# Six of 32 head pairs multiply float32 probabilities with v as loaded, sums of both heads inverted together, and a new order of work

## The chip, the cores and the metric

The kernel runs on one core of a Trainium2 chip. The metric is the device time of one execution in microseconds (us). The engines are TensorE (PE, and PEld for its weight loads), VectorE (DVE), ScalarE (ACT), GpSimd (POOL) and SyncE (SP), which issues the transfers.

## The reference

Attention with a decay, and behind it a token and channel mixer with residual additions:

```python
scores = (q @ k.T) / sqrt(64)
cum = cumsum(log(clip(f, 1e-4, 1)))
scores = where(causal, -1e9, scores + cum[:, None] - cum[None, :])
attn = exp(scores - max(scores)); attn /= sum(attn) + 1e-9
x = attn @ v                                    # 8 batches, 8 heads, 576 tokens, 64 wide
u = x + (relu(x.T @ w_tok1) @ w_tok2).T         # 576 -> 256 -> 576
out = u + relu(u @ w_ch1) @ w_ch2               # 512 -> 1536 -> 512
```

All of it is float32. The weights come as float64 words and are decoded on the chip.

## The kernel before

The 64 heads are worked in 32 pairs (`n2`); the heads of a pair sit on the two halves of the 128 partitions, so that matmuls with 64 rows of each can run side by side. Four pairs are one batch of 8 heads, and after every second pair half a batch goes through the mixer (`mixer`, `joint`, `tok2`, and in the second half `ch1` and `ch2`). The channels that the mixer leaves out are done after attention with late weights (`unit`, then `plain_up`, `plain_down`, and products with fewer multiplications).

Most products run in rounded float32 (F32R): an operand is split into a high part, rounded by a copy, and a low part, which is the subtraction of the two (`hi_act` L508 on ACT, `lo_dve` L517 on DVE, `lo_pool` L514 on POOL). One float32 product then becomes two or three rounded ones. The scores of the first four pairs (`FQ=4`) are the exception: they use q and k as loaded, in float32.

A pair goes through these steps. Scores by `score` (L768), six pieces a head, each with one more rounded product for the decay (`cd`). Row minima by `rmin` (L782, DVE). Exponentials with row sums by `expo` (L786, ACT). Per head, 1e-9 is added to the sums and they are inverted (`rec1` L812, `rec2` L815, DVE), and five instructions normalise the probabilities (`norm` L820, POOL). Transpositions in three groups (`trs` L838, PE). For each group and head a copy to the high part (L508, ACT) and a low part (L517, DVE) into `pt`. Then `avs` (L883) multiplies `pt` with `vv`, in which v's high and low parts stand side by side in 128 columns (split at L742 by ACT and L514 by POOL), high `pt` first and then low `pt`; the results for v's high and low parts land on two halves of the partitions, and a copy by ACT (L898) with an addition by DVE (L902) joins them in `xt`. The block of the first 64 tokens has a lone 64-column product per head (`low`, L871); the second head's must wait for the first's, and stands at the head of the third group.

Weights are decoded by `decode`: a scaling on ACT (L588), two shifts or masks on DVE (L592, L596), a multiplication (L600), an addition (L604, POOL for the early weights and DVE for the late), a last merge (L608), then high and low parts.

The order of each engine's work is a table of numbers (`ORDER`) written out beforehand. `Plan.run` takes the operations of each engine in just that order, and picks the buffers as they come free by its own cost figures; `PORT` tells it from which batch on an operation marked `port=True` (decode steps on DVE) and any operation on POOL are kept from overlapping in its reckoning. On the chip the engines wait for each other by semaphores alone.

Buffers matter in two places. `part` is four float32 tiles that `ch2` uses for results on their way out. And the weights of the late part take over the room of attention's tiles in two steps, `gate0` when `raw`, `hl`, `vr` and `pr` are done with, `gate1` for `vv`, `pt` and `xn`.

Of the kernel before, what the change touches and what calls it, by code (L numbers as in the profile page):

```python
# [1709 lines left out]
```

## Time and profile before

| | us |
|---|---|
| median of 3 runs | 1044.23 |
| lowest, highest | 1042.71, 1045.01 |
| profiled execution | 1044.65 |
| its span | 1042.9 |
| busy: PE, PEld | 989.0, 895.0 |
| busy: DVE, ACT, POOL | 866.4, 629.9, 441.3 |

Busy time is a union over the whole span. The stages differ: attention runs up to about 541 us, the late weights are decoded up to about 674 us, and the rest is products with them. So a share of the whole says little, and the rows below are taken by stretch. The granted clock is given as a share of 2.4 GHz; TensorE has two levels, 1.2 and 2.4 GHz, and 0.76 is a mean of both. Idle time of an engine is put down to what ended it.

### The profile page before, as it was taken

Reading aid. Unit: us, or ns where it says so; the run is one execution under the profiler, and the core shown is the slowest. Engines: PE = TensorE matmul, PEld = TensorE weight load, DVE = VectorE, ACT = ScalarE, POOL = GpSimd, SP = SyncE. Lnnn points to the kernel's source line nnn. Section 1 sums busy time; section 2 is a strip of 40 time slices with the busy share of each in tenths; the row PEclk is TensorE's granted clock in tenths of the full one; section 3 lists DMA queues with packets and bytes.
Section 4 is the critical chain, followed back from the end, with each engine's and each line's share of the span. In section 5 each row is a group of like instructions: output and inputs, shape, how many; then the busy total and the mean of one; then the engine's idle time right before and its main releaser. Section 6 shows DMA issues by size and latency. Waiting matters only on the chain.

```text
span 1042.9 us, 26969 instructions
## 1 busy us (share of the span) xinstructions
PE 989.0 (95%) x10030; PEld 895.0 (86%) x10030; DVE 866.4 (83%) x2221; ACT 629.9 (60%) x1582; POOL 441.3 (42%) x519
## 2 busy tenths in 40 slices
PE   7579899999999999999987999999999999999998
PEld 5468899999999999999987888888888888888887
DVE  7998988788787887879788999958967994996487
ACT  5768688898897988889884544524513431442242
POOL 6767758778686877867731000012002200110210
PEclk9668899999999999999997999999999999999999
DMA  5331123333432232332416989999799879988884
GB/s 187 113 104 56 36 68 106 94 96 104 139 93 104 70 120 71 92 110 85 139 60 212 334 268 334 310 308 349 218 315 320 299 235 308 315 256 250 266 301 147
DMA packets 125859, 192.78 MB, mean 185 GB/s; under 512 B 18976, under 2 KB 77088, under 8 KB 124704
## 3 DMA queue, kind: packets, MB, share of 16 engines
q1 hardware_dynamic: 125632, 190.91, 56.5%
q8 instruction: 79, 1.29, 0.5%
q14 instruction: 52, 0.43, 0.1%
q10 hardware_dynamic: 96, 0.15, 0.0%
HBM read 144.34 MB, written 46.66 MB: 183 GB/s over the span
## 4 chain that ended last, share of the span: by engine, by line
PE 78%; DVE 14%; ACT 4%; DMA 2%; issue 1%; POOL 0%; SPq 0%; DVEq 0%; ACTq 0%
PE bank L1349 18%; PE bank L883 8%; PE bank L768 7%; PE bank L1165 6%; PE bank L1166 6%; PE bank L1167 6%; PE bank L1232 6%; PE bank L1230 6%; PE bank L1231 6%; PE bank L838 4%; DVE pr L782 3%; DVE xt L902 2%; DVE d_g L592 1%; ACT pr L786 1%; DVE pt L517 1%
## 5 line engine op out<-in xcount | busy, mean ns | idle before, releaser
L820 POOL TENSOR_SCALAR pr<-pr,rec 128x576 f32<-128x576 f32 (+4 forms) x320 | 169.8, 551 | 104.6 <-DVE rec L815 85.3
L786 ACT ACTIVATE pr<-pr,nmin 64x64 f32<-64x64 f32 (+4 forms) x320 | 177.2, 559 | 19.2 <-DVE nmin L782 18.6
L517 DVE TENSOR_TENSOR pt<-bank,pt 128x512 fp32r<-128x512 f32 x192 | 124.8, 682 | 16.4 <-ACT pt L508 15.4
L782 DVE CUSTOM_DVE_ANT_0 pr<-bank,mask 128x320 f32<-128x320 f32 (+3 forms) x320 | 124.8, 426 | 5.6 <-PE bank L768 4.9
L883 PE MATMUL bank<-pt,vv 64*128 64x512 f32 (+7 forms) x1152 | 115.6, 335 | 4.6 <-DVE pt L517 4.5
L508 ACT ACTIVATE pt<-bank 128x512 fp32r<-128x512 f32 x192 | 105.2, 597 | 19.8 <-PE bank L838 14.5
L768 PE MATMUL bank<-hl 64*128 64x320 f32 (+4 forms) x1008 | 105.5, 307 | 5.0 <-DVE nmin L782 3.7
L883 PEld LDWEIGHTS bank<-pt,vv 64*128 64x128 f32 x1152 | 102.4, 197 | 7.2 <-DVE pt L517 6.1
L768 PEld LDWEIGHTS bank<-hl 64*128 64x128 f32 x1008 | 87.4, 188 | 8.8 <-DVE nmin L782 5.4
L838 PE MATMUL bank<-ident,pr 64*128 64x64 f32 x1536 | 70.8, 232 | 14.7 <-DVE nmin L782 6.4
L838 PEld LDWEIGHTS bank<-ident,pr 64*128 64x128 f32 x1536 | 64.1, 145 | 17.4 <-POOL pr L820 14.9
L508 ACT ACTIVATE hid<-h 128x480 fp32r<-128x480 f32 x77 | 45.8, 602 | 54.1 <-PE bank L1231 36.9
L768 PE MATMUL bank<-cd,sel 64*128 64x320 f32 (+4 forms) x384 | 74.0, 340 | 4.1 <-DVE cd L551 4.1
L902 DVE TENSOR_TENSOR xt<-bank,xt 64x512 f32<-64x512 f32 (+1 forms) x128 | 57.2, 453 | 24.3 <-ACT xt L898 21.7
L514 POOL TENSOR_TENSOR hl<-raw,hl 128x1152 fp32r<-128x1152 f32 x28 | 75.0, 2678 | 1.5
L1349 PE MATMUL bank<-xn,t1h 64*128 64x256 f32 x512 | 63.6, 313 | 2.9 <-DVE ring L517 1.9
L1258 POOL TENSOR_TENSOR d_g<-d_g 128x480 f32<-128x480 f32 x4 | 5.1, 1280 | 142.6 <-DMA d_g<-pd 127.6
L786 ACT ACTIVATION_READ_ACCUMULATOR pr<-pr,nmin 128x1 f32 (+1 forms) x320 | 62.6, 196 | 0.0
L1349 PE MATMUL bank<-ring,w2h 64*128 64x288 f32 x512 | 59.9, 297 | 1.6 <-DVE ring L520 1.5
L1349 PE MATMUL bank<-ring,w1h 64*128 64x288 f32 x512 | 59.5, 305 | 1.3 <-POOL ring L514 1.3
L508 ACT ACTIVATE ring<-xt 128x576 fp32r<-128x576 f32 (+3 forms) x64 | 39.3, 632 | 34.5 <-DVE xt L1429 19.4
L898 ACT ACTIVATE xt<-bank 64x64 f32<-64x64 f32 (+1 forms) x128 | 50.3, 404 | 16.3 <-PE bank L883 12.7
(241 smaller groups left out, 3076.0 us busy)
## 6 DMA issues: line engine op xcount, KB each, us to landing
pw<-wd SPq DMA_DIRECT2D x280, 256.0 KB, 4.1
raw<-in_qk SPq DMA_DIRECT2D x28, 576.0 KB, 3.9
d_raw<-in_w_ch SPq DMA_DIRECT2D x80, 128.0 KB, 3.7
...
```

The source lines that it names most:

```text
L508: nc.scalar.activation(out, in_, func, scale=scale)
L514: nc.gpsimd.tensor_tensor(out, in_, asf(hi), op=ALU.subtract)
L517: nc.vector.tensor_tensor(out, in_, asf(hi), op=ALU.subtract)
L768: nc.tensor.matmul(at(buf)[:, of : of + w], q, k, start=(x == 0), stop=(x == len(passes)))
L782: nc.vector.tensor_tensor_reduce(o, x, y, -1.0 / D**0.5, first, op0=ALU.add, op1=ALU.min, accum_out=c0[:m, col : col + 1])
L786: nc.scalar.activation(x, x, AF.Exp, bias=E["nmin"][sm][:m, t : t + 1], scale=-1.0, accum_out=E["sums"][sm][:m, t : t + 1])
L820: nc.gpsimd.tensor_scalar(x, x, E["rec"][sm][:m, t // 2, t % 2 : t % 2 + 1], 0.0, op0=ALU.mult, op1=ALU.add)
L838: nc.tensor.transpose(at(ps[s])[:, k * D : (k + 1) * D], at(pr)[r, x, :, :].rearrange("p a b -> p (a b)"), E["ident"][r, r])
L883: nc.tensor.matmul(at(av[s])[:, 512 - w :], at(vv)[r, vblk(j), :], at(pt)[r, z, c : c + w], start=(z, gi, i) == (0, 0, 0), stop=(z, gi, i) ...
L902: "DVE", d_dve(n), lambda ps=ps, o=o, n=n, f=f, xt=xt, me=me, pp=pp: nc.vector.tensor_tensor(at(xt)[me, pp, o : o + n], at(ps)[me, f : f + ...
L1165: nc.tensor.matmul(o, wt[:, 0, :], h_, start=(first and k == 0), stop=False, skip_group_check=True)
L1349: last[s] = nc.tensor.matmul(at(ps[s ^ z])[:, : width[0]], a, m, start=(z == 0 and i == 0), stop=(z == 1 and i == len(todo[s]) - 1), skip_ ...
```

## The change

Pairs 0 to 3, 30 and 31 (`FV`) skip the splitting of v and of the transposed probabilities. Each transposed group is copied once, by ACT, into a float32 tile `pf`, which is made of two of the four `part` tiles, so two groups have room at a time. `avs` multiplies it in float32 with `vr`, v as loaded, 64 columns wide, in one product where there were two; one copy by ACT brings the result to `xt`, and DVE's additions are gone.

In all pairs the sums of both heads stand in one tile and are inverted by one `rec1` and one `rec2`, for which the last exponential of either head must be done; all ten normalisations follow from them. The lone 64-column product of the second head moves from the head of the third group to its end.

`PORT` is 0, so the planner keeps port operations and POOL apart from the first batch on; some of its cost figures are new, and the order table of every engine is new.

```diff
 PRM = dict(
-    FILL=36, F1=2, FQ=4, n_raw=1, ...
+    FILL=36, F1=2, FQ=4, FV=(0, 1, 2, 3, 30, 31), n_raw=1, ...
-PORT = 6
+PORT = 0
 ORDER = dict(
     PE=(
-        "10:32 189 192 197 206 279 42 262 43 265 270 44 229 234 239 45 363 244 371 366 245:2 380 302 307 312 317:3 439 "
+        "10:36 195 187 190 204 246 249 263 254 225 228 234 231 235:2 284 287 333 341 350 336 293 290 294 392 295 400 "
...
-        fq = n2 < FQ
+        fq, fv = n2 < FQ, n2 in PRM["FV"]
...
-        p.op("ACT", d_act((2 * NS - 1) * D, False), lambda vv=vv, vr=vr: nc.scalar.activation(at(vv)[:, :, 0:D], at(vr), AF.Copy), ...)
-        p.op("POOL", d_ptt((2 * NS - 1) * D), lambda vv=vv, vr=vr: lo_pool(at(vv)[:, :, D:], at(vr), at(vv)[:, :, 0:D]), ...)
+        if not fv:
+            p.op("ACT", ...)
+            p.op("POOL", ...)
...
+        sm = n2 % 2
+        def rec1(sm=sm):
+            nc.vector.tensor_scalar(E["rec"][sm][:, :, :2], E["sums"][sm].rearrange("p (a b) -> p a b", b=3), 1e-9, None, op0=ALU.add)
...
+        p.op("DVE", 78, rec1, rd=[("sums", 2 * sm + s, t) for s in (0, 1) for t in range(NS)], wr=[("rec", sm)])
+        p.op("DVE", 136, rec2, wr=[("rec", sm)])
         for s in (0, 1):
-            p.op("DVE", 72, rec1, rd=[("sums", sm, t) for t in range(NS)], wr=[("rec", sm)])
-            p.op("DVE", 100, rec2, wr=[("rec", sm)])
             for t in (4, 3, 2, 1, 0):
-                p.op("POOL", d_pts(end[t], 1), lambda t=t, f=norm: f(t), rd=[("rec", sm)], wr=[(pr, s, t)], bufs=[pr])
+                p.op("POOL", d_pts(end[t], 1), lambda t=t, s=s, f=norm: f(t, s), rd=[("rec", sm)], wr=[(pr, s, t)], bufs=[pr])
...
-            ps, pt = [Buf("bk"), Buf("bk")], Buf("pt")
+            ps, pt = [Buf("bk"), Buf("bk")], Buf("pf" if fv else "pt")
...
+                if fv:
+                    o = lambda pt=pt, s=s: at(pt).rearrange("p (k s x) -> p k s x", s=2, x=D)[:, :, s, :]
+                    p.op("ACT", d_act(512), lambda src_=src_, o=o: nc.scalar.activation(o(), src_(), AF.Copy), rd=[ps[s]], wr=[(pt, 0, s)], bufs=[ps[s], pt])
+                    continue
...
+                Z, M = ((0,), D) if fv else ((0, 1), P)
+                def left(r, j):
+                    return at(vr)[r, vblk(j), :] if fv else at(vv)[r, vblk(j), :]
+                def right(b, r, z, c, w):
+                    return at(b)[r, c : c + w] if fv else at(b)[r, z, c : c + w]
...
-                if gi == 2:
-                    low(1)
                 for i, (j, c, w) in enumerate(seq):
-                    for z in (0, 1):
+                    for z in Z:
                         for s in (0, 1):
...
-                                at(av[s])[:, 512 - w :], at(vv)[r, vblk(j), :], at(pt)[r, z, c : c + w],
+                                at(av[s])[:M, 512 - w :], left(r, j), right(pt, r, z, c, w),
...
+                if gi == 2:
+                    low(1)
...
+                if fv:
+                    p.op(
+                        "ACT", d_act(n) + 60, lambda ps=ps, o=o, n=n, f=f, xt=xt, me=me, pp=pp: nc.scalar.activation(at(xt)[me, pp, o : o + n], at(ps)[:D, f : f + n], AF.Copy),
+                        rd=tok, wr=[(xt, 2 * pp + s, o)], bufs=[ps, xt],
+                    )
+                    continue
...
+    k["pf"] = [(("part", 2 * i), ("part", 2 * i + 1)) for i in (0, 1)]
```

How the new table moves instructions shows best in three places. The first is DVE in pair 0, where the sums of head 0 (`sums_85`) are inverted; `pr` are the probabilities of a pair, `nmin` its row minima, `d_g` weights in decode. Before:

```order
L812 TENSOR_SCALAR rec_89<-sums_85 128x3x2
L782 ISA pr_178,nmin_82<-bank_68,mask 64x64
L782 ISA nmin_82 64x1
L815 RECIPROCAL rec_89<-rec_89 128x3x2
L608 SCALAR_TENSOR_TENSOR d_g_161<-d_raw,d_g_161 128x256
L592 TENSOR_SCALAR d_g_162<-d_g_162 128x256
L782 ISA pr_178,nmin_82<-bank_64,mask 128x3x64
L782 ISA nmin_82 128x1
L596 TENSOR_SCALAR d_g_162<-d_g_162 128x256
```

On DVE at the same step of pair 0 now:

```order
L588 TENSOR_SCALAR d_g_162<-d_g_162 128x256
L596 SCALAR_TENSOR_TENSOR d_g_161<-d_raw,d_g_161 128x256
L592 TENSOR_SCALAR d_g_162<-d_g_162 128x256
L807 TENSOR_SCALAR rec_89<-sums_85 128x6x2
L810 RECIPROCAL rec_89<-rec_89 128x6x2
L778 ISA pr_176,nmin_83<-bank_64,mask 128x3x64
L778 ISA nmin_83 128x1
L778 ISA pr_176,nmin_84<-bank_65,mask 128x5x64
```

The inversion is twice as wide, it stands behind all row minima of pair 0 instead of between them, and it is followed by minima of pair 1 (`pr_176`). The second place is further down on DVE, where stood the first low halves of the probabilities (`pt`), between decode steps and minima of pair 1. Before:

```order
L600 SCALAR_TENSOR_TENSOR d_g_161<-d_raw,d_g_161 128x256
L782 ISA pr_179,nmin_84<-bank_66,mask 128x3x64
L782 ISA nmin_84 128x1
L517 TENSOR_TENSOR pt_182<-bank_63,pt_182 128x8x64
L592 TENSOR_SCALAR d_g_162<-d_g_162 128x288
L782 ISA pr_179,nmin_83<-bank_65,mask 128x3x64
L782 ISA nmin_83 128x1
L596 TENSOR_SCALAR d_g_162<-d_g_162 128x288
```

After the inversion of pair 1 DVE now goes on with decode and the minima of pair 2:

```order
L807 TENSOR_SCALAR rec_90<-sums_86 128x6x2
L810 RECIPROCAL rec_90<-rec_90 128x6x2
L604 SCALAR_TENSOR_TENSOR d_g_161<-d_raw,d_g_161 128x256
L596 SCALAR_TENSOR_TENSOR d_g_162<-d_raw,d_g_162 128x256
L778 ISA pr_175,nmin_82<-bank_70,mask 128x5x64
L778 ISA nmin_82 128x1
```

No low half stands there any more. The third place is PE in the middle of attention, behind the last score of pair 16 (`hl` are q and k, split; `cd,sel` the decay). Before:

```order
L768 MATMUL bank_64<-hl_177 128x192
L768 MATMUL bank_65<-hl_177 128x192
L768 MATMUL bank_64<-cd,sel 128x192
L768 MATMUL bank_65<-cd,sel 128x192
L883 MATMUL bank_63<-pt_182,vv_181 128x320
L883 MATMUL bank_68<-pt_182,vv_181 128x320
```

PE behind the last score of pair 16 now:

```order
L764 MATMUL bank_64<-hl_173 128x64
L764 MATMUL bank_65<-hl_173 128x64
L764 MATMUL bank_64<-cd,sel 128x64
L764 MATMUL bank_65<-cd,sel 128x64
L1365 MATMUL bank_70<-xn_182,t1h 128x256
L1365 MATMUL bank_68<-xn_182,t1h 128x256
L1365 MATMUL bank_70<-xn_182,t1l 128x256
L1365 MATMUL bank_68<-xn_182,t1l 128x256
```

Before, the multiplications of pair 15 by v followed at once, and 106 matmuls stood between that score and the first transposition of pair 16; now the mixer's token product and the transpositions of pair 15 come first, and 229 stand between.

## Rows read from the trace of the kernel before

**Rows 1.** Table by stretch: length, PE, PEld, DVE, ACT, POOL busy; clock, DMA.

```profile
0.00:15.00 15.00, 9.08 (x76) 5.91 (x76) 8.48 (x19) 5.00 (x7) 8.50 (x18) 1.00 0.65 214
15.00:116.00 101.00, 76.31 (x840) 66.31 (x840) 94.72 (x278) 76.54 (x214) 73.41 (x90) 0.76 0.28 88
116.00:541.00 425.00, 417.30 (x6596) 407.61 (x6598) 351.53 (x1173) 356.85 (x1003) 306.89 (x372) 0.99 0.30 97
541.00:674.00 133.00, 122.15 (x870) 106.31 (x869) 127.27 (x286) 64.89 (x129) 6.13 (x4) 0.95 0.86 279
674.00:1042.90 368.90, 364.12 (x1656) 308.83 (x1654) 284.44 (x469) 126.65 (x231) 46.32 (x36) 1.00 0.86 278
```

**Rows 2.** Chain that ended last, 0 to 116 us, its shares.

```profile
by line: DVE pr L782 14.0%; DVE d_g L592 11.6%; PE bank L883 11.2%; issue 5.8%; DVE d_g L600 5.5%; DVE pt L517 4.8%; DVE d_g L596 4.8%; DVE xt L902 4.5%; PE bank L768 4.2%; ACT pt L508 3.1%; DVE d_g L608 3.0%; DMA d_raw<-in_w_tok 2.6%; POOL
```

**Rows 3.** Timeline, 105 to 121 us: start, length, engine, line, instruction.

```profile
110.12 4.63 DVE L592 TENSOR_SCALAR d_g<-d_g 128x512 uint32<-128x512 uint32 x1
...
113.06 1.40 POOL L514 TENSOR_TENSOR vv<-vr,vv 128x576 fp32r<-128x576 f32 x1
...
116.00 1.19 PE L883 MATMUL bank<-pt,vv 64*128 64x320 f32 x16 [2.25 <-DVE pt L517]
```

**Rows 4.** Groups on DVE, 0 to 116 us: count, busy us, mean ns, idle.

```profile
L517 DVE TENSOR_TENSOR pt<-bank,pt 128x512 fp32r<-128x512 f32 x27 | 17.7, 678 | 0.2
L592 DVE TENSOR_SCALAR d_g<-d_g 128x256 uint32<-128x256 uint32 (+2 forms) x17 | 16.1, 947 | 5.6 <-ACT d_g L588 5.5
L600 DVE SCALAR_TENSOR_TENSOR d_g<-d_raw,d_g 128x256 f32<-128x256 uint32 (+2 forms) x16 | 11.9, 741 | 0.1
L596 DVE TENSOR_SCALAR d_g<-d_g 128x256 uint32<-128x256 uint32 (+2 forms) x16 | 8.8, 549 | 0.1
L608 DVE SCALAR_TENSOR_TENSOR d_g<-d_raw,d_g 128x256 uint32<-128x256 uint32 (+2 forms) x15 | 8.4, 561 | 0.0
L902 DVE TENSOR_TENSOR xt<-bank,xt 64x512 f32<-64x512 f32 (+1 forms) x16 | 7.1, 453 | 2.0 <-ACT xt L898 1.2 <-PE bank L871 0.7
...
L815 DVE RECIPROCAL rec<-rec 128x6 f32<-128x6 f32 x10 | 1.8, 181 | 0.0
```

**Rows 5.** DVE while POOL rests: timeline at 6 us; a group, 520 to 680.

```profile
6.64 0.29 DVE L592 TENSOR_SCALAR d_g<-d_g 128x256 uint32<-128x256 uint32 x1 [5.45 <-ACT d_g L588]
...
7.55 0.42 DVE L600 SCALAR_TENSOR_TENSOR d_g<-d_raw,d_g 128x256 f32<-128x256 uint32 x1
...
L600 DVE SCALAR_TENSOR_TENSOR tmp<-d_raw,tmp 128x512 f32<-128x512 uint32 x6 | 4.1, 684 | 0.0
```

**Rows 6.** Timeline of PE: float32 scores, then products with v.

```profile
60.61 0.60 PE L768 MATMUL bank<-xt 64*128 64x256 f32 x4
...
61.16 0.70 PE L768 MATMUL bank<-xt 64*128 64x320 f32 x4
...
62.18 0.80 PE L768 MATMUL bank<-xt 64*128 64x320 f32 x3 [0.16 <-DVE xt L902]
...
62.97 0.48 PE L768 MATMUL bank<-xt 64*128 64x192 f32 x3
...
404.13 0.36 PE L1349 MATMUL bank<-xn,t1h 64*128 64x256 f32 x2
...
405.70 0.31 PE L883 MATMUL bank<-pt,vv 64*128 64x320 f32 x1
...
408.93 0.35 PE L1349 MATMUL bank<-t2h,ring 64*128 64x288 f32 x2
```

**Rows 7.** Timeline around the normalisation of pair 16, 296 to 302 us.

```profile
296.51 2.56 POOL L820 TENSOR_SCALAR pr<-pr,rec 128x576 f32<-128x576 f32 x5 [0.54 <-DVE rec L815]
...
300.01 2.57 POOL L820 TENSOR_SCALAR pr<-pr,rec 128x576 f32<-128x576 f32 x5 [0.94 <-DMA raw<-in_qk]
...
302.00 0.65 PE L838 MATMUL bank<-ident,pr 64*128 64x64 f32 x16
```

More of the change, by code (lines that the diff above doesn't have):

```diff
@@ L313 @@
     START = dict(PE=3000, DVE=900, ACT=1900, POOL=1810, SP=700)
-    FIFO = ("ring", "xt", "part", "pr", "hl", "vv", "raw", "vr", "pt", "xn", "av", "hid", "hidB", "pw", "sg", "sg2", "uh", "uh2", "H", "st", "wq", "q", "rr", "g2", "d_raw", "d_g", "qf")
+    FIFO = ("ring", "xt", "part", "pr", "hl", "vv", "raw", "vr", "pt", "pf", "xn", "av", "hid", "hidB", "pw", "sg", "sg2", "uh", "uh2", "H", "st", "wq", "q", "rr", "g2", "d_raw", "d_g", "qf")
     def __init__(self):
@@ L488, in d_act @@
     def d_act(n, ps=True, ptr=0):
-        return 0.833 * n + (51 if ps else 93) + 93 * ptr + (130 if n > 512 else 0)
+        return 0.833 * n + (51 if ps else 93) + 93 * ptr + (130 if ps and n > 512 else 0)
     def d_dve(n, fast=False):
@@ L497, in d_ptt @@
     def d_ptt(n):
-        return 150 + 2.1 * n
+        return 145 + 2.157 * n
     def at(b):
@@ L542, in decay @@
             p.op("ACT", 900, lambda q=q: ld(nc.scalar, q), wr=[("f", q)], bufs=[w], lat=2500)
-        p.op("DVE", d_dve(S, True), lambda: nc.vector.tensor_scalar(row(0), row(0), 1e-4, 1.0, op0=ALU.max, op1=ALU.min), rd=[("f", q) for q in range(4)], wr=["f"], bufs=[w])
+        p.op("DVE", d_dve(S, True), lambda: nc.vector.tensor_scalar(row(0), row(0), 1e-4, 1.0, op0=ALU.max, op1=ALU.min), rd=[("f", q) for q in range(4)], wr=["f"], bufs=[w], port=True)
         p.op("ACT", d_act(S, False) + 1300, lambda: nc.scalar.activation(row(0), row(0), AF.Ln), wr=["f"], bufs=[w])
         p.op(
-            "DVE", d_dve(S), lambda: nc.vector.tensor_tensor_scan(row(1), row(0), row(2), 0.0, op0=ALU.add, op1=ALU.add),
-            rd=["f", "zero"], wr=["c"], bufs=[w],
+            "DVE", 1270, lambda: nc.vector.tensor_tensor_scan(row(1), row(0), row(2), 0.0, op0=ALU.add, op1=ALU.add),
+            rd=["f", "zero"], wr=["c"], bufs=[w], port=True,
         )
-        p.op("DVE", d_dve(S, True), lambda: nc.vector.tensor_scalar(E["cd"], row(1), 1.0, None, op0=ALU.mult), rd=["c"], wr=["cd"], bufs=[w])
+        p.op("DVE", d_dve(S, True), lambda: nc.vector.tensor_scalar(E["cd"], row(1), 1.0, None, op0=ALU.mult), rd=["c"], wr=["cd"], bufs=[w], port=True)
         p.op(
             "DVE", d_dve(S), lambda: nc.vector.scalar_tensor_tensor(E["cd"], asf(E["cd"]), E["lows"], row(1), op0=ALU.mult, op1=ALU.add),
-            rd=["c"], wr=["cd"], bufs=[w],
+            rd=["c"], wr=["cd"], bufs=[w], port=True,
         )
@@ L608, in s6 @@
             nc.vector.scalar_tensor_tensor(g, high, 0x80000000, g, op0=ALU.bitwise_and, op1=ALU.bitwise_or)
-        m2, m1 = (1.2, 1.1) if p.batch < PORT else (1.0, 1.0)
         p.op("ACT", d_act(w, False), s1, rd=rd, wr=[gb], bufs=[rb, gb])
-        p.op("DVE", d_dve(w, True) * (m2 if late else 1.8), s2, wr=[gb], bufs=[gb], port=True)
-        p.op("DVE", d_dve(w, True) * (m2 if late else 1.8), s3, rd=[gb], wr=[(gb, 1)], bufs=[gb], port=True)
-        p.op("DVE", d_dve(w) * (m1 if late else 1.3), s4, port=True, rd=rd, wr=[(gb, 1)], bufs=[rb, gb])
+        p.op("DVE", d_dve(w, True) , s2, wr=[gb], bufs=[gb], port=True)
+        p.op("DVE", d_dve(w, True) , s3, rd=[gb], wr=[(gb, 1)], bufs=[gb], port=True)
+        p.op("DVE", d_dve(w) , s4, port=True, rd=rd, wr=[(gb, 1)], bufs=[rb, gb])
         p.op("DVE" if late else "POOL", d_dve(w) if late else d_ptt(w), s5, port=True, rd=[(gb, 1)], wr=[gb], bufs=[gb])
@@ L785, in expo @@
             m, x = size[t], prob(t, s)
-            nc.scalar.activation(x, x, AF.Exp, bias=E["nmin"][sm][:m, t : t + 1], scale=-1.0, accum_out=E["sums"][sm][:m, t : t + 1])
+            nc.scalar.activation(x, x, AF.Exp, bias=E["nmin"][sm][:m, t : t + 1], scale=-1.0, accum_out=E["sums"][sm // 2][:m, sm % 2 * (NS + 1) + t : sm % 2 * (NS + 1) + t + 1])
         for ts in ((4,), (5,), (3, 0), (2, 1)):
@@ L796, in build @@
                     p.op(
-                        "DVE", d_dve(where[0][t][3]), lambda t=t, s=s, sm=sm, f=rmin: f(t, s, sm), rd=[ps[s]] + ([("nmin", sm, NS)] if t == 5 else []),
+                        "DVE", d_dve(where[0][t][3]) + 68 * (t == 5), lambda t=t, s=s, sm=sm, f=rmin: f(t, s, sm), rd=[ps[s]] + ([("nmin", sm, NS)] if t == 5 else []),
                         wr=[(pr, s, t), ("nmin", sm, NS if t == 4 else min(t, 4))], bufs=[ps[s], pr],
@@ L863, in build, with avs @@
                 k += len(y)
-            def avs(seq=seq, pt=pt, pts=pts, av=av, ax=ax, vv=vv, gi=gi, last=last):
+            def avs(seq=seq, pt=pt, pts=pts, av=av, ax=ax, vv=vv, vr=vr, fv=fv, gi=gi, last=last):
+                Z, M = ((0,), D) if fv else ((0, 1), P)
[3 more added lines that the diff above has]
+                    return at(b)[r, c : c + w] if fv else at(b)[r, z, c : c + w]
                 def low(s):
@@ L876, in avs @@
                     low(0)
-                if gi == 2:
-                    low(1)
                 for i, (j, c, w) in enumerate(seq):
-                    for z in (0, 1):
+                    for z in Z:
                         for s in (0, 1):
@@ L1555, in attn_mixer_kernel @@
     )
-    for nm, shape in (("nmin", [P, NS + 1]), ("sums", [P, NS + 1]), ("rec", [P, NS // 2 + 1, 4])):
+    for nm, shape in (("nmin", [P, NS + 1]), ("sums", [P, 2 * NS + 2]), ("rec", [P, NS + 1, 4])):
         E[nm] = [const.tile(shape, F32, name=f"{nm}{i}") for i in range(4)]
@@ L1595, in attn_mixer_kernel @@
     tiles(mixp, "d_g", [P, 2, C], U32, n_("d_g"))
-    tiles(mixp, "part", [P, S], F32, n_("part"))
+    parts = mixp.tile([P, 4, S], F32, name="part")
+    E["part"] = {(("part", i),): parts[:, i, :] for i in range(4)}
+    E["pf"] = {(("part", 2 * i), ("part", 2 * i + 1)): parts[:, 2 * i : 2 * i + 2, :].rearrange("p a b -> p (a b)")[:, :1024] for i in (0, 1)}
     att = [tc.tile_pool(name=f"att{x}", bufs=1, side=side) for x, side in enumerate(("right", "left"))]
```

36 lines of the change are left out of this document (17 added, 19 removed), and 452 rows, old and new, of tables (ACT, DVE, PE, POOL).

## The prediction

> **What bounds the kernel now.** I read the table by stretch first, then the chain of waits of the first stretch, then the groups of instructions on VectorE there, and last the timelines where a row needed a neighbour. The first multiplication by v of pair 4 starts at 116.00 us; up to there TensorE is busy for 9.08 + 76.31 = 85.4 us and VectorE for 8.48 + 94.72 = 103.2 us [rows 1]. From 15 us on VectorE hardly pauses (94.72 of 101), and the granted clock is 0.76: with levels of half and full, 48% of that stretch was at 1.2 GHz. The chain of waits says the same: its largest parts are VectorE's row minima (L782) and the weight decode (L592, L600, L596) [rows 2]. From 116 to 541 us TensorE is busy for 417.30 of 425 at clock 0.99: the rest of attention is TensorE's, with 7.7 us to be had at most. From 541 to 674 us, where the late weights are decoded, both are nearly full (VectorE 127.27, TensorE 122.15 of 133), and the last 369 us are TensorE's again [rows 1]. So an edit pays in the first 116 us, and later only through TensorE's own work.
>
> Part of VectorE's time there is no work. At 110.12 one 512-wide shift takes 4.63 us and ends only behind GpSimd's split of v, which starts at 113.06 and takes 1.40; the first multiplication by v of pair 4 had waited 2.25 us when it started [rows 3]. The four decode groups take 16.1 + 11.9 + 8.8 + 8.4 = 45.2 us in 64 instructions [rows 4]. Undisturbed, a 256-wide one takes 0.29 or 0.42 and a 512-wide multiplication 0.684 [rows 5]. Most are narrow, so I take 0.42 each, 27 us, and 18 us of stretch.
>
> The Trainium skill says why (SBUF — State Buffer, section SBUF: two separate sides): VectorE, with two inputs in SBUF or in a two-port mode, and GpSimd hold one port pair by turns, the second fully blocked. By that rule the new order saves only where the two no longer meet; this trace agrees with the 4.63 us.
>
> **The change part by part.** I follow it to the first multiplication by v of pair 4, and count what both orders have done by then.
>
> *VectorE.* The low halves of pairs 0 to 3 go (six a pair), and so do their 16 additions into xt. Before had spent 17.7 us on 27 low halves (three are pair 4's) and 7.1 on the additions [rows 4]; the new order has only 5 low halves there, all of pair 4, 3.4 us. Six reciprocals instead of ten save 0.7. The order has 47 decode instructions ahead of the mark for 64: 17 x 0.42 = 7.1 less, and 5 less of the stretch if it falls in proportion. Two more small steps of the mixer and four more additions, at the 0.453 of an addition [rows 4], cost 2.7. Together 103.2 - 24.8 + 3.4 - 0.7 - 7.1 - 5 + 2.7 = 72 us; with none of the remaining stretch met it would be 59, with all of today's 77.
>
> *GpSimd and ScalarE.* GpSimd is busy for 8.50 + 73.41 = 81.9 us up to the mark [rows 1]; four splits of v go (1.40 each [rows 3]), eight decode steps come later and one q/k split earlier, which I set against each other: about 76. ScalarE has 5.00 + 76.54 = 81.5 [rows 1]; its copies of the probabilities stay one for one, four copies of v and some decode steps go: 76 to 81. Neither sets the end if TensorE needs more.
>
> *TensorE.* A product of a pair's probabilities with v is now one float32 pass over 2,944 columns where it was two rounded ones. The old form takes from 405.70 to 408.93, 3.23 us, or 1.10 ns a column. The nearest float32 products are the scores of pair 3 at full clock: 256 columns start at 60.61 and the next at 61.16, 320 at 62.18 and the next at 62.97 [rows 6]. Taking off the rounded product inside each at half of 1.10 ns, 1.6 and 1.9 ns a column remain. So a pair costs 4.7 to 5.6 us. I take the dearer, 5.6, 2.4 more than now, since the products with v are as narrow or narrower; as the upper end 2.2 ns, once more the difference of the two, 6.5. Up to the mark that is 4 x 2.4 = 9.7.
>
> A rule against the change stands in FP8 and Floating Point Precision, section TensorE Precision Notes, of the Trainium skill: true float32 takes 4 passes of the array. By it a pair would cost twice the old form, 6.46 us, and the sum below would come out 6 x 0.8 = 4.9 us later; the score rows are cheaper than that, and I go by them.
>
> Work of TensorE up to the mark, at full clock: of the 85.4 busy us, 48% of 76.31 ran at half speed, so 18 us are lost to the clock and 67 remain. The new order has two more score groups (576 columns in four rounded products at 0.55 ns, 1.3) and four more mixer phases ahead of the mark (one runs from 404.13 to 405.70, 1.6 [rows 6], so 6.5): 67 + 1.3 + 6.5 + 9.7 = 84.5. With VectorE at 72 and the others at 76 to 81, TensorE has the most to do. What it still waits for: about 6 us before 15 us (9.08 of 15 busy now; the decay chain is still first), some 8 while pair 0 goes through exponentials, sums, normalisation and copy once, and 4 of half clock around both. The 8 and the 4 are estimates, from 30.6 us of idle time and 18 lost to the clock up to the mark now, most of it behind a VectorE that has 31 us less to do. That is 84.5 + 6 + 8 + 4 = 102.5 for 116.
>
> *Given back later.* The two score groups and four phases done early (7.8) no longer stand behind the mark. Pairs 30 and 31 cost 2 x 2.4 = 4.8 more.
>
> *Sums of both heads at once.* In pair 16 head 0's five normalisations start at 296.51 behind their reciprocal, head 1's at 300.01, and the transpositions at 302.00, while GpSimd still works on the last [rows 7]. Now none starts before the later reciprocal, so five more (2.56 us) stand between it and the transpositions. Queued behind the one waiting addition on VectorE are row minima of the next pair. I cost it at nothing: ahead of the first transposition of pair 16 the order has 229 matmuls after its last score for 106 before, among them 75 of a mixer, three phases of 1.6 us. If that cover is gone it costs 2.6 us in each of 27 pairs.
>
> *The rest.* The lone 64-column product at the end of its group is the same matmul, and its wait for the other head's product was met before too: zero. In 541 to 674 us VectorE loses the low halves and additions of pair 31, up to 5 us; against it, the weights' buffers open behind pair 31's products with v as loaded, no longer behind a split copy of v: up to one pair's 5.6 us later for the decode. I take zero for the stage. In the late stage TensorE is at 364.12 of 368.90 with the same products: zero.
>
> **Sum** against the profiled execution, 1044.65 us (span 1042.9; the median of the runs, 1044.23, is 0.4 lower, so the same figure serves): 1044.65 - (116 - 102.5) - 7.8 + 4.8 = 1028.2, so **1028 us**. With no wait but the first 6 us the mark is at 90.5, 1016; with float32 at 2.2 ns it is 5 more than forecast. Its own range is 1017 to 1039.
>
> **The rivals.**
> 1. *The stretch stays in the way, no gain.* The order was written out with GpSimd and VectorE kept apart, but engines run by semaphores, and an order that slips makes them meet again. For it: 4.63 us in one instruction [rows 3], and decode now stands among pairs 5 to 9 as well, where row minima queue behind it. Against it: four splits of v less. If 13 us of stretch fall on the path, the mark is at 116 and the time 1028 + 13 = 1041 to 1042. This is also what the skill's page on SBUF would make of an order that doesn't part them. Chance 0.13.
> 2. *Slower: normalisation comes late.* The cover named above is used up in half of the lag, 1.3 us in each of 27 pairs: 1028 + 35 = 1063. It decides from the point at which transpositions wait for GpSimd in every pair between 116 and 541 us, where TensorE has 7.7 us of idle time in all now. For it: only 1.99 us lie between the second half's start and the transpositions [rows 7], so nothing spare is in the chain itself. Against it: 123 more matmuls ahead of them. Chance 0.10.
> 3. *More than forecast.* A lighter VectorE lets TensorE close half of its 7.7 us of idle time in attention and 6 of the 11 in the decode stage [rows 1], and the start goes to 98: 1028 - 4 - 6 - 5 = 1013. For it: VectorE is fuller than TensorE in the decode stage, and loses work just ahead of it. Against it: the weights there are decoded by the same instructions as before, and they are nearly all of its 127.27 us. Chance 0.12.
>
> **How the numbers follow.** The forecast has 0.65. What a measurement of this kernel can tell from no change is about 0.2%, 2 us: 1042.1 to 1046.3. Faster: 0.65 + 0.12, and 0.06 of rival 1's 0.13; same: its other 0.07; slower: rival 2's 0.10. The range for 8 in 10 reaches from 1012, which leaves the lower half of rival 3 outside, to 1043, which leaves out rival 2 and little of rival 1.
>
> **What would show it.** Right: pair 4's first multiplication by v at 98 to 108 us, TensorE's clock in the first 116 us above 0.85, VectorE's busy time up to the mark near 72, float32 products of a pair in 4.7 to 5.6 us, and 116 to 541 us with no more idle time than now. Wrong: transpositions that wait for GpSimd after every pair (rival 2); a decode instruction of 2 us and more ahead of row minima (rival 1); or a float32 product above 6.5 us a pair.

## The result and the profile after

| | before | after |
|---|---|---|
| median of 4 runs, us | 1043.47 | 1025.16 |
| lowest, highest | 1042.15, 1045.01 | 1024.23, 1029.15 |
| profiled execution | 1044.65 | 1024.95 |
| its span | 1042.9 | 1023.1 |

The ratio is 0.983, with a 95% interval of 0.980 to 0.986. The forecast was 1028 us in a range of 1012 to 1043, with a chance of 0.83 for faster. Intervals reach 0.2 to 0.3% to either side; where those of two kernels overlap, the text goes by the traces, of which each shows one execution.

The table by stretch of the kernel after, cut at the same events as [rows 1]: the first product with v of pair 4 (the mark), the first with v of pair 31, and so on. Columns as there.

```profile
0.00:15.00 15.00, 12.77 (x111) 8.99 (x113) 6.91 (x23) 5.05 (x7) 4.97 (x16) 1.00 0.62 207
15.00:100.80 85.80, 75.33 (x879) 58.87 (x877) 57.72 (x215) 69.72 (x204) 63.04 (x83) 0.90 0.31 95
100.80:523.00 422.20, 412.64 (x6519) 399.04 (x6516) 346.65 (x1116) 356.86 (x1005) 307.66 (x376) 0.99 0.31 100
523.00:655.00 132.00, 123.43 (x888) 106.97 (x889) 124.00 (x282) 65.73 (x132) 5.85 (x4) 0.97 0.86 279
655.00:1023.10 368.10, 361.70 (x1644) 306.79 (x1642) 282.73 (x466) 127.33 (x231) 54.69 (x36) 1.00 0.86 278
```

The mark is at 100.8 instead of 116.0: 15.2 of the 19.8 us that the span lost. From the mark to pair 31's first product with v (at 541.5 us before, 523.0 after) it is 422.2 for 425.5, and from there to the end 500.1 for 501.4. VectorE is busy for 6.91 + 57.72 = 64.6 us up to the mark, where it was 103.2, and the clock from 15 us on is 0.90 for 0.76. TensorE is idle for 100.8 - 88.1 = 12.7 us up to the mark; it was 30.6.

The chain that ended last, 0 to 100.8 us of the kernel after, its shares:

```profile
by line: PE bank L890 20.1%; PE bank L764 14.1%; PE bank L1365 10.7%; POOL pr L815 9.4%; PE bank L834 7.0%; DVE pr L778 6.4%; DVE d_g L604 5.9%; DMA vr<-in_v 4.6%; issue 2.8%; SPq L570 2.1%; SPq L724 1.6%; DVE d_g L596 1.6%; SPq L733 1.5%; 
```

In [rows 2] VectorE led. Now TensorE does, with the products with v (L890) first. Of VectorE only the row minima (L778) and one decode step (L604) are left among the large parts.

VectorE's decode groups, 0 to 100.8 us, which answer to [rows 4] (L588, L592, L596, L604 were L592, L596, L600, L608; count, then busy us, mean ns, idle):

```profile
L604 DVE SCALAR_TENSOR_TENSOR d_g<-d_raw,d_g 128x256 uint32<-128x256 uint32 (+1 forms) x11 | 9.7, 885 | 0.0
L596 DVE SCALAR_TENSOR_TENSOR d_g<-d_raw,d_g 128x256 f32<-128x256 uint32 (+1 forms) x12 | 6.2, 520 | 0.2
...
L588 DVE TENSOR_SCALAR d_g<-d_g 128x256 uint32<-128x256 uint32 (+1 forms) x12 | 3.5, 292 | 10.8 <-ACT d_g L584 10.7
L592 DVE TENSOR_SCALAR d_g<-d_g 128x256 uint32<-128x256 uint32 (+1 forms) x12 | 3.4, 293 | 0.1
```

They take 22.8 us in 47 instructions for 45.2 in 64. The shift and the mask (L588, L592) are at the undisturbed 0.29 [rows 5]; the time that GpSimd still adds to decode steps (the prediction's "stretch") sits in L604, and there in few instructions. The timeline of one of them, at 16 us (start, length, engine, line, instruction, idle time before it and who ended it):

```profile
16.39 2.62 POOL L510 TENSOR_TENSOR hl<-raw,hl 128x1152 fp32r<-128x1152 f32 x1
...
16.41 2.88 DVE L604 SCALAR_TENSOR_TENSOR d_g<-d_raw,d_g 128x256 uint32<-128x256 uint32 x1
...
20.44 1.43 PE L764 MATMUL bank<-xt 64*128 64x320 f32 x3 [3.50 <-DVE nmin L778]
```

The step starts 0.02 us behind GpSimd's split of pair 4's q and k and ends only behind it, 2.88 us for the 0.41 of its neighbours. Row minima queue behind it, and TensorE's scores behind those, 3.50 us. That is what the prediction had named as a sign against itself, "a decode instruction of 2 us and more ahead of row minima". Of VectorE's instructions of 0.95 us and more I count those that overlap one of GpSimd's: 14 up to the mark before, 3 after (at 16.41, 52.16 and 93.69 us).

### The profile page after: what moved, and what is told of

Read it like the earlier page. It is cut to its first block, busy times and chain, and to the rows that moved or that the text cites. A ratio compares the mean times of both kernels' runs of the same rounds, so it can differ in the third digit from the quotient of the medians.

```text
span 1023.1 us, 26774 instructions
## 1 busy us (share of the span) xinstructions
PE 985.9 (96%) x10030; PEld 880.6 (86%) x10030; DVE 818.0 (80%) x2097; ACT 624.7 (61%) x1576; POOL 436.2 (43%) x513
## 4 chain that ended last, share of the span: by engine, by line
PE 79%; DVE 11%; POOL 3%; DMA 2%; ACT 2%; issue 2%; SPq 1%; DVEq 0%; ACTq 0%; POOLq 0%
PE bank L1365 17%; PE bank L890 9%; PE bank L764 7%; PE bank L1248 6%; PE bank L1247 6%; PE bank L1246 6%; PE bank L1181 5%; PE bank L1182 5%; PE bank L1183 5%; PE bank L834 5%; POOL pr L815 2%; DVE pr L778 2%; DVE xt L918 1%; PE bank L1042 1%; PE bank L1063 1%
## 5 line engine op out<-in xcount | busy, mean ns | idle before, releaser
L782 ACT ACTIVATE pr<-pr,nmin 128x576 f32<-128x576 f32 (+4 forms) x320 | 176.9, 559 | 11.0 <-DVE nmin L778 10.3
L778 DVE CUSTOM_DVE_ANT_0 pr<-bank,mask 128x320 f32<-128x320 f32 (+3 forms) x320 | 125.3, 428 | 28.0 <-PE bank L764 16.0
L513 DVE TENSOR_TENSOR pt<-bank,pt 128x512 fp32r<-128x512 f32 x156 | 102.1, 684 | 13.0 <-ACT pt L504 11.7
L1274 POOL TENSOR_TENSOR d_raw<-d_raw 128x480 f32<-128x480 f32 x15 | 26.3, 1756 | 161.5 <-DMA d_raw<-ud 114.3
L890 PE MATMUL bank<-pt,vv 64*128 64x320 f32 (+7 forms) x936 | 92.2, 318 | 0.0
L504 ACT ACTIVATE pt<-bank 128x512 fp32r<-128x512 f32 x156 | 85.0, 602 | 10.2 <-PE bank L834 6.2
L890 PEld LDWEIGHTS bank<-pt,vv 64*128 64x128 f32 x936 | 81.6, 186 | 1.4
L764 PE MATMUL bank<-cd,sel 64*128 64x320 f32 (+4 forms) x384 | 77.8, 330 | 0.4 <-DVE cd L547 0.4
L1365 PE MATMUL bank<-t2h,ring 64*128 64x288 f32 x512 | 63.5, 304 | 3.2 <-DVE pt L513 0.9
L1365 PE MATMUL bank<-xn,t1h 64*128 64x256 f32 x512 | 57.1, 293 | 3.7 <-DVE xn L513 2.4
L1248 PE MATMUL bank<-hid,pw 128*128 128x480 f32 x152 | 58.0, 382 | 1.6 <-DVE hid L513 1.5
```

The costliest lines, as they stand in the source:

```text
L504: nc.scalar.activation(out, in_, func, scale=scale)
L513: nc.vector.tensor_tensor(out, in_, asf(hi), op=ALU.subtract)
L764: nc.tensor.matmul(at(buf)[:, of : of + w], q, k, start=(x == 0), stop=(x == len(passes)))
L778: nc.vector.tensor_tensor_reduce(o, x, y, -1.0 / D**0.5, first, op0=ALU.add, op1=ALU.min, accum_out=c0[:m, col : col + 1])
L782: nc.scalar.activation(x, x, AF.Exp, bias=E["nmin"][sm][:m, t : t + 1], scale=-1.0, accum_out=E["sums"][sm // 2][:m, sm % 2 * (NS + 1) + t ...
L890: nc.tensor.matmul(at(av[s])[:M, 512 - w :], left(r, j), right(pt, r, z, c, w), start=(z, gi, i) == (0, 0, 0), stop=(z, gi, i) == (Z[-1], ...
```

## The experiments

Each kernel starts from the changed kernel or, where "old order" is said, has the instruction order of the kernel before. In each, an instruction that the other order didn't have was put in where its inputs are there by the planner's times; no order was laid out anew for any of them. Times are medians; ratios are to the kernel before, measured beside.

| kernel | us | ratio, 95% interval | mark | pair 31 |
|---|---|---|---|---|
| before | 1043.5 | 1 | 116.0 | 541.5 |
| changed | 1025.2 | 0.983 (0.980 to 0.986) | 100.8 | 523.0 |
| old_order_fv | 1048.3 | 1.006 (1.003 to 1.008) | 120.0 | 544.4 |
| fv_last | 1044.4 | 1.000 (0.998 to 1.002) | 116.4 | 539.8 |
| fv_first | 1029.1 | 0.987 (0.984 to 0.989) | 100.3 | 520.9 |
| fv_31 | 1027.5 | 0.983 (0.981 to 0.985) | 100.5 | 521.1 |
| old_merged | 1102.0 | 1.056 (1.053 to 1.059) | 122.2 | 600.7 |
| new_sep | 1026.7 | 0.984 (0.982 to 0.987) | 100.4 | 522.0 |
| low_head | 1023.2 | 0.980 (0.978 to 0.982) | 99.8 | 520.3 |
| fv_twice | 1047.0 | 1.004 (1.002 to 1.006) | 119.4 | 542.8 |
| low_back | 1031.9 | 0.989 (0.985 to 0.992) | 105.3 | 527.7 |
| warm | 1033.5 | 0.991 (0.988 to 0.993) | 103.9 | 530.1 |
| split_behind | 1027.9 | 0.984 (0.982 to 0.985) | 99.7 | 521.8 |
| split_behind_warm | 1026.3 | 0.982 (0.980 to 0.984) | 101.2 | 522.6 |

**The work without the order.** Float32 in pairs 0 to 3, the order of before.

```diff
-FV=(0, 1, 2, 3, 30, 31)
+FV=(0, 1, 2, 3)     # sums per head, low(1) at the head, old ORDER
```

> The order of before, with only pairs 0 to 3 multiplying float32 probabilities with v as loaded (no split of v, low halves or additions for them; sums per head and the lone product as before). What had to move for the fewer buffers: the loads of v of pairs 1 to 5, the first product of these pairs, the split of v of pairs 4 and 5. Theory A, the gain is the work taken off VectorE (24.8 us in the first 116): the first product with v of pair 4 starts at 100 to 106 us and the time is 1030 to 1034. Theory B, the gain is the new order: it starts at 112 us or later and the time is 1038 to 1046.

It came out at 1048.3, 4 us slower than before, with the mark at 120.0. The row from 15 us up to the mark, and the timeline in the 7 us ahead of it:

```profile
15.00:120.00 105.00, 81.64 (x840) 61.00 (x838) 70.01 (x237) 73.75 (x210) 67.78 (x86) 0.82 0.28 82
```

```profile
113.09 2.65 POOL L512 TENSOR_TENSOR hl<-raw,hl 128x1152 fp32r<-128x1152 f32 x1
...
113.87 4.92 DVE L590 TENSOR_SCALAR d_g<-d_g 128x512 uint32<-128x512 uint32 x1
...
115.70 1.40 POOL L512 TENSOR_TENSOR ring<-xt,ring 128x576 fp32r<-128x576 f32 x1
...
117.07 1.43 POOL L512 TENSOR_TENSOR vv<-vr,vv 128x576 fp32r<-128x576 f32 x1
```

VectorE did lose its work: 70.01 and 8.37 ahead of 15 us make 78.4 us for 103.2. But the mark didn't follow. Ten of its instructions still lie across GpSimd's, the shift of 4.63 us [rows 3] is there again with 4.92, behind three GpSimd instructions in a row (as it was before, from 109.05 us on; [rows 3] shows the last of them), and TensorE is idle for 27.6 us, nearly as before. Theory A falls. Part of this is the edit's own: float32 holds the one `vr` buffer up to the pair's last product, so the load of pair 4's v lands late, ScalarE waits 3.04 us for it with pair 3's copies to `xt` queued behind, and TensorE 2.41 us for those.

```profile
106.90 0.68 ACT L740 ACTIVATE vv<-vr 128x576 fp32r<-128x576 f32 x1 [3.04 <-DMA vr<-in_v]
...
107.74 1.01 PE L1383 MATMUL bank<-ident,xt 64*128 64x64 f32 x18 [2.41 <-ACT xt L910]
```

**The order without the work.** The new order, with pairs 0 to 3 in the rounded form.

```diff
-FV=(0, 1, 2, 3, 30, 31)
+FV=(30, 31)
```

> The changed kernel, in its new order, with pairs 0 to 3 in the rounded form again (float32 products in 30 and 31 alone; splits, low halves and additions put in by the time their inputs are there). Theory A, the gain is work taken off VectorE and GpSimd: the first product with v of pair 4 starts at 118 us or later, the time is 1042 or more. Theory B, the new order makes the gain by itself: 1025 to 1035.

It takes as long as the kernel before (1044.4), as theory A has it; its mark, 116.4, is 1.6 us ahead of where that theory began. (Its profile shows the slowest of eight executions, 1049.5 us; behind pair 31 it is 7 us longer than the changed kernel.) The row from 15 us up to its mark, and the longest wait of TensorE there (us in total, times, longest):

```profile
15.00:116.40 101.40, 78.47 (x884) 70.25 (x880) 81.80 (x256) 72.63 (x208) 67.89 (x87) 0.80 0.26 79
```

```profile
PE bank L891 <- DVE pt L514: 6.8, 6, 2.0
```

Only five VectorE instructions of 0.95 us and more overlap one of GpSimd's there, so the order does part them. VectorE has 88.9 us to do, and TensorE's products with v wait for the low halves. So neither half of the change gains anything alone, as tried here: +4 and 0 us, and together -18. Which of the many moves in the new table counts was not taken apart.

**Pairs 30 and 31.** Both in the rounded form, and then pair 30 alone.

```diff
-FV=(0, 1, 2, 3, 30, 31)
+FV=(0, 1, 2, 3)        # fv_first
+FV=(0, 1, 2, 3, 31)    # fv_31
```

> The changed kernel with pairs 30 and 31 in the rounded form again (their splits, low halves and additions put in by the time their inputs are there; v of pair 31 loaded behind the split of pair 30). Theory A, as predicted, float32 in these two costs 2.4 us each and gives back nothing: 1020 to 1021. Theory B, VectorE without their 12 low halves and 8 additions starts the late weights earlier: 1026 to 1032.

> The changed kernel with pair 30 in the rounded form and pair 31 left in float32. With both rounded the time was 1029.1, with both in float32 1025.2. Theory A, what the two give is VectorE's room just ahead of the late weights, which only pair 31 takes up; pair 30 then only costs its 2.3 us of TensorE: 1021 to 1024. Theory B, pair 30's low halves and additions hinder too: 1026 to 1029.

The medians (1029.1, 1027.5, and 1025.2 with both in float32) overlap in their intervals; the traces tell more. From pair 31's first product with v to the first product of the next stage, first of fv_first, then of fv_31:

```profile
520.90:562.20 41.30, 32.31 (x370) 28.71 (x370) 38.59 (x85) 22.37 (x48) 5.84 (x4) 0.83 0.59 190
```

```profile
521.10:560.40 39.30, 30.86 (x373) 26.14 (x371) 32.95 (x76) 22.61 (x48) 5.82 (x4) 0.91 0.61 198
```

The changed kernel has 39.1 us there. Pair 31 in float32 takes 5.6 us off VectorE, the clock is at 0.91 for 0.83, and this part is 2.0 us shorter although the float32 products are the dearer ones. Pair 30 in float32 costs in the traces: from its first product with v to pair 31's it takes 15.0 us in the changed kernel for 13.6 in fv_first and 13.4 in fv_31. By these rows theory A of fv_31 holds, but its median lies in theory B's range, and its trace is of the fastest of its four executions (1024.4); so whether float32 in pair 30 gains or costs in all is not shown.

**Sums of both heads at once.** In the old order (no other work changed), and taken apart again in the new one.

```diff
 # old_merged: FV=(), low(1) at the head, old ORDER, normalisations behind the common inversion
-        for s in (0, 1):
-            p.op("DVE", 72, rec1, rd=[("sums", sm, t) for t in range(NS)], wr=[("rec", sm)])
...
+        p.op("DVE", 78, rec1, rd=[("sums", 2 * sm + s, t) for s in (0, 1) for t in range(NS)], wr=[("rec", sm)])
 # new_sep: the reverse, in the new order
```

> The order of before, with only the sums of both heads inverted at once (all normalisations of a pair then stand behind the later head's exponentials). Theory A, the merging needs cover between a pair's last score and its first transposition, which the old order (106 matmuls at pair 16) lacks: 0.5 to 2.6 us in each of 27 pairs, 1058 to 1114. Theory B, merging costs nothing anywhere: 1041 to 1046.

> The changed kernel with the sums inverted for each head by itself again (head 0's inversion where its sums are there, head 1's where the common one stood, normalisations in the same row). Theory A, the cover hides the merging: 1023 to 1028. Theory B, the transpositions that still wait for normalisations (3.4 us in 101 to 523 us) are the merging's price: 1020 to 1022. Theory C, VectorE misses the 64 instructions saved: 1030 and more.

The old order loses 58 us by it; in the new one it makes no difference that can be measured. The transpositions' group of the kernel before (116 to 541 us), of old_merged (122 to 600) and of the kernel after (101 to 523): busy, mean ns, idle ahead of them.

```profile
L838 PE MATMUL bank<-ident,pr 64*128 64x64 f32 x1296 | 57.9, 226 | 0.8 <-DVE xn L517 0.6
```

```profile
L833 PE MATMUL bank<-ident,pr 64*128 64x64 f32 x1296 | 65.1, 241 | 31.5 <-POOL pr L814 15.8 <-DVE nmin L777 14.8 <-DVE xn L512 0.3
```

```profile
L834 PE MATMUL bank<-ident,pr 64*128 64x64 f32 x1280 | 55.7, 228 | 3.1 <-POOL pr L815 1.0 <-DVE xt L918 0.9 <-DVE nmin L778 0.7
```

And the stretch of old_merged:

```profile
122.20:600.70 478.50, 439.21 (x6602) 425.39 (x6604) 350.73 (x1122) 358.12 (x1003) 304.96 (x372) 0.94 0.27 86
```

It is 53 us longer than [rows 1] has it. TensorE is idle for 39.3 us, 31.6 more than before, 1.2 in each of 27 pairs; and it is busy for 21.9 more with the same products, at a clock of 0.94 for 0.99. Half of the transpositions' 31.5 us is ended by a normalisation (15.8), half by a row minimum (14.8).

The 106 and 229 matmuls that the prediction counted as cover are those of pair 16, and their number doesn't decide. Over pairs 5 to 31 it is 107 to 292 in the old order and 132 to 342 in the new one; pairs with 198 to 206 wait 0.4 to 1.9 us in old_merged, and the new order's pair 10, with 132, doesn't wait. What parts the two is the time from the end of the common inversion to the first transposition. Pair 16 of old_merged, then pair 10 of the kernel after:

```profile
325.76 0.23 DVE L809 RECIPROCAL rec<-rec 128x12 f32<-128x12 f32 x1
...
329.99 0.37 PE L833 MATMUL bank<-ident,pr 64*128 64x64 f32 x2 [1.51 <-POOL pr L814]
```

```profile
189.08 0.22 DVE L810 RECIPROCAL rec<-rec 128x12 f32<-128x12 f32 x1
...
193.48 0.66 PE L834 MATMUL bank<-ident,pr 64*128 64x64 f32 x16
```

Four us pass in both, but in the first 1.5 of them are a wait. Taking the wait off, the old order leaves 1.7 to 3.6 us in 21 of the 27 pairs, and 20 of these wait; the new one leaves 4.1 us and more in all 27, and five wait at all, 0.95 us at most. By these rows it is this room that makes the merging free; no run changed the room alone.

**The lone product.** Back at the head of its group.

```diff
+                if gi == 2:
+                    low(1)
                 for i, (j, c, w) in enumerate(seq):
...
-                if gi == 2:
-                    low(1)
```

> The changed kernel with the second lone 64-column product back at the head of its group, the only edit. Theory A, as predicted, where it stands costs nothing: 1023 to 1028. Theory B, at the head it waits for the first lone product's end with the rest of the group behind it, up to 0.3 us (its own length) in each of 32 pairs: 1030 to 1035.

At 1023.2 us its interval overlaps that of the changed kernel; pair 31 begins 2.7 us earlier. So the move gains nothing that can be measured, and may cost up to 2 us: near the zero of the forecast, on the other side if at all.

**What sets the start now.** TensorE's float32 products doubled, and VectorE's low halves brought back.

```diff
-                Z, M = ((0,), D) if fv else ((0, 1), P)
+                Z, M = ((0,) * (2 if n2 < 4 else 1), D) if fv else ((0, 1), P)   # fv_twice
...
+                    if n2 < 4:                                                   # low_back
+                        p.op("DVE", d_dve(512), ... lo_dve(at(lo)..., src_(), dst()), ...)
```

> The changed kernel with every float32 product with v of pairs 0 to 3 issued twice (their sums are then not the reference's). In the trace of the changed kernel these products take 6.50, 5.13, 5.13 and 5.25 us from start to start, 22 in all. Theory A, TensorE sets the pace up to the mark: 1037 to 1047. Theory B, it waits for the chain of exponentials, sums and normalisations anyway: 1025 to 1030.

> The changed kernel with the 24 low halves of the probabilities of pairs 0 to 3 computed on VectorE again, into a tile that nobody reads: 24 x 0.68 = 16.4 us. Theory A, VectorE is no longer the bound up to the mark (64.6 of 100.8 us busy): 1025 to 1031. Theory B, it still is: 1037 to 1042.

Twice the products cost 21.9 us (1047.0 for 1025.2), 18.6 of them at the mark: up to there TensorE is busy for 106.8 us in place of 88.1 and idle for as long as before, 12.6. The clock from 15 us on is 0.95 for 0.90, so part of the 22 us is given back. 16.4 us more on VectorE cost 6.8, of which 4.5 are at the mark, between the ranges of the two theories. So TensorE sets the start now, as forecast; VectorE has cover for more than half of those 16.4 us, but not for all.

**The clock.** Small matmuls in TensorE's two pauses ahead of pair 0's transpositions.

```diff
+            if n2 == 1 and ts == (4,):
+                for i in range(40 + 40):
+                    p.op("PE", ..., nc.tensor.matmul(at(ps[0])[:64, 448:496], E["ident"][:, :64], E["ident"][:, :48], ...))
```

> The changed kernel with 80 small matmuls (64 x 48, into unused columns of a bank) in TensorE's two pauses ahead of pair 0's transpositions, 40 before the last but one score group of pair 1 and 40 before the transpositions. In the changed kernel the clock is at half from 19.5 to 36.1 us, with 12.2 us of TensorE's work in it. Theory A, the pauses bring the clock down and the slow work after them stands on the path: the clock stays at full and the time is 1019 to 1022. Theory B, the clock stays full but the chain behind sets the pace: 1024 to 1027. Theory C, the small matmuls don't hold the clock: 1025 to 1030.

At 1033.5 us it is outside all three ranges. The dose was wrong: each is two matmuls in the trace, and the first part had to wait for the bank it writes to. Their rows, and the transpositions behind them:

```profile
21.14 5.48 PE L792 MATMUL bank<-ident 128*64 128x48 f32 x64 [2.85 <-DVE nmin L779]
29.07 4.87 PE L792 MATMUL bank<-ident 128*64 128x48 f32 x80
33.87 0.71 PE L838 MATMUL bank<-ident,pr 64*128 64x64 f32 x16
```

The clock is at half only from 21.4 to 24.8 us (19.3 to 36.3 in the changed kernel), but the transpositions come at 33.9 for 28.9. What the clock gives back is visible all the same: pair 0's products end 8.1 us behind the first transposition instead of 10.9. Of the 9.7 us by which the profiled span is longer, 3.1 are at the mark; another 3.9 arise between the mark and pair 29, with the same busy time, and why stays open.

**The one meeting that is left on the path.** GpSimd's split put behind the step that it had blocked, and then with small matmuls in the pause.

```diff
     POOL=(
-        "0 52 61 55 508:2 64 70 ...
+        "0 52 61 55 508 64 509 70 ...
 # split_behind_warm, besides: FILL=36 becomes 76, the 40 ahead of pair 0's first transposition
```

> The changed kernel with two GpSimd instructions exchanged: the low half of pair 4's q and k (2.6 us, 16.39 to 19.02 in the changed kernel) behind the low half of the second weight piece instead of ahead of it. In the changed kernel VectorE's last decode step of that piece starts 0.02 us after the split and ends only at 19.30, 2.9 us for 0.4. Theory A, that one meeting stands on the path: the step ends by 17, the first transposition of pair 0 starts at 25.5 to 27 (28.9 before) and the time is 1021 to 1023.5. Theory B, ScalarE's exponentials of pair 0 follow each other anyway: the first transposition at 28 or later, 1024 to 1027.

> The same exchange, and 40 more of the small matmuls that fill the start (each two of 64 x 48 in the trace, 62 ns each, 5 us in all) between pair 1's last scores and pair 0's first transposition. Theory A, they lie in TensorE's pause and hold the clock, so pair 0's products with v run at full clock: the first group of pair 1's products starts 2 to 4 us earlier than without them, time 1017 to 1021. Theory B, they reach beyond the pause: the first transposition comes later than without them by what they overrun, the time is that of the exchange alone or up to 4 us more.

The timeline of split_behind:

```profile
16.21 0.41 DVE L604 SCALAR_TENSOR_TENSOR d_g<-d_raw,d_g 128x256 uint32<-128x256 uint32 x1
...
17.77 0.94 PE L764 MATMUL bank<-xt 64*128 64x320 f32 x3 [1.03 <-DVE nmin L778]
...
20.03 2.71 POOL L510 TENSOR_TENSOR hl<-raw,hl 128x1152 fp32r<-128x1152 f32 x1
...
20.45 2.44 DVE L592 TENSOR_SCALAR d_g<-d_g 128x256 uint32<-128x256 uint32 x1
...
27.78 0.37 PE L834 MATMUL bank<-ident,pr 64*128 64x64 f32 x2 [7.00 <-POOL pr L815]
```

The step is at 0.41 us, and the scores behind it start 2.7 us earlier. But the split now meets the mask of the next weight piece, 2.44 us for 0.28, and the inversion of the sums queues behind that. The first transposition is 1.1 us earlier, between the two theories, the mark 1.1, and of the total nothing can be told. The meeting has moved.

With the small matmuls the clock between 24 and 28 us is 1.00, where it was 0.51 in split_behind and 0.50 in the changed kernel. They fit the pause, and the transposition still waits:

```profile
21.05 5.18 PE L557 MATMUL bank<-ident 128*64 128x48 f32 x80
28.13 0.28 PE L835 MATMUL bank<-ident,pr 64*128 64x64 f32 x2 [1.90 <-POOL pr L816]
```

By 32 us, in the pauses that follow, the clock is at half again (0.50 from 32 to 36), so pair 0's products gain nothing. Theory A falls (pair 1's products start at 44.3 us for 43.5), and so does B's reason, since the matmuls end ahead of the wait. No version here beats the changed kernel by more than the intervals; low_head has the lowest median.

## Why the prediction was right, and where not

**The mark**, forecast 102.5, came at 100.8, and each engine's load came out near its term. VectorE: 64.6 for 72. What was too high is the time that GpSimd adds to decode steps, of which I had let 13 of 18 us stay; 22.8 us in 47 instructions at my own 0.42 leave 3. TensorE at full clock: 88.1 busy less about 6 lost between 19.3 and 36.3 us, 82 for 84.5. Its waits with the clock: 12.7 + 6 = 19 for the 18 of the forecast. Their parts are off and cancel: 2.2 before 15 us for 6, 10.5 behind it for 8, 6 of half clock for 4. That the sum met the mark to 2 us is partly luck. (Two products in the working are a tenth off, 6 x 0.8 and 4 x 1.6; they move nothing.)

**The reason given for it was half of it.** The prediction put the fewer waits down to "a VectorE that has 31 us less to do", and took the new order for a matter of 7.8 us of work done ahead. VectorE's loss of work alone moved the mark by +4 us, the order alone by 0.4. In the old order the engines stand in rows laid out for a full VectorE: it was idle for 42 us up to the mark of old_order_fv, 14.7 of them for ScalarE's first step of a decode (5.5 before), and ten of its steps still met GpSimd. The sum came out because both were in it, not because each term was worth what it said.

**Float32 products.** The rows of pair 1 in the kernel after, at full clock, with what stands between them:

```profile
44.69 1.73 PE L890 MATMUL bank<-part,vr 64*64 64x320 f32 x16
46.35 0.71 PE L834 MATMUL bank<-ident,pr 64*128 64x64 f32 x16
47.00 0.27 PE L880 MATMUL bank<-part,vr 64*64 64x64 f32 x1
...
48.77 0.81 PE L764 MATMUL bank<-xt 64*128 64x320 f32 x4
...
49.65 1.93 PE L890 MATMUL bank<-part,vr 64*64 64x512 f32 x8
...
51.63 1.02 PE L764 MATMUL bank<-xt 64*128 64x448 f32 x4
```

From start to start 1.66 + 1.77 + 1.98 = 5.4 us, forecast 5.6 in a range of 4.7 to 5.6. The dearer of the two score rows was the right neighbour. That is 1.7 times the old form. The Trainium skill (FP8 and Floating Point Precision, section TensorE Precision Notes) states four passes for true float32; the estimate of 6.46 us drawn from it, twice the old form, is not borne out.

**Work ahead and pairs 30 and 31.** Forecast -7.8 from the mark on and +4.8 for the two pairs. From the mark to pair 31 the forecast is 425.5 - 7.8 + 2.4 = 420.1; it was 422.2, since TensorE's idle time there rose from 7.7 to 9.6 us, against the sign that I had named. Pair 30 cost 1.4 to 1.6 in the traces for its 2.4. Pair 31's 2.4 is the step with the wrong sign: that part is shorter with it in float32, by 2.0 us. I had put VectorE's gain there at zero, "up to 5 us" against a later start of the decode.

**Merged sums and the lone product**, both at zero: right by new_sep, and within 2 us by low_head. The reason for the first was half right: TensorE's work does cover the merging, but it counts from the inversion on, and the matmuls behind the last score, taken at one pair, don't tell it. **The late stages**, at zero: from pair 31 to the end 500.1 us for 501.4.

**The rivals.** The first (GpSimd's meetings with decode stay, 1041 to 1042) is not what happened, but its mechanism is part of what old_order_fv shows, and one such meeting is left on the path, 2.88 us for 0.41 when GpSimd starts 0.02 us earlier. The Trainium skill has the two hold one port pair by turns (SBUF — State Buffer, section SBUF: two separate sides); the trace agrees with that 2.88 us. The second (normalisation late, 1.3 us in each of 27 pairs, 1063) didn't happen either; where its cover is missing it costs 1.2 us a pair in waits, as priced, and two thirds as much again in busy time at the lower clock, which the price left out. The third (more than forecast) got the start at 100.8, not 98, and its half of the idle time in attention didn't come.

**What would show it**: mark in 98 to 108, clock above 0.85 and float32 in 4.7 to 5.6 us held; VectorE near 72 and no more idle time in attention didn't. Of the signs of being wrong one did show, rival 1's decode instruction of 2 us and more ahead of row minima (2.88 us at 16.41): the meeting that split_behind moved but did not remove.

## What to carry to other kernels

Where the order of every engine's work is written out, work taken off the bound engine may be worth nothing until the order is laid out anew for it, and a new order nothing while that work is still there; here both were so, and the two have to be priced together. A dependency that is made coarser (one inversion for two heads) is free as long as independent work of the next engine covers it. That cover is to be counted in time, from the event that comes late, and in every pair; a count of instructions at one pair misleads. And a wait of TensorE is to be priced above its length where the clock falls behind it.

## What the runs showed of the chip

- VectorE's decode steps and GpSimd exclude each other to the instruction: 2.88 us for 0.41 at 16.41 us, and, when the split was moved, 2.44 for 0.28 in a step with one input in place of two. It goes the other way too: in the kernel before, two normalisations at 74.87 us took 2.85 us, where five take 2.56 [rows 7], while two decode steps beside them ran undisturbed at 0.68 and 0.67. An order can part the two on paper and lose by 0.02 us on the chip.
- Idle time of TensorE brings more than itself: in old_merged 31.6 us of waits came with 21.9 us more of busy time for the same products, at a clock of 0.94 for 0.99. In the kernel after, TensorE pauses for 3.50 us ahead of 20.44 us; in that pause, at 19.3, the granted clock goes to half, and it is full again only from 36.3 us on.
- A float32 product of 64 rows and 64 columns of v takes 5.4 us a pair where two rounded passes with 128 columns take 3.23 [rows 6].
